# Softmax of a decode attention kernel: per-head exps on ACT replaced by chunked bias adds on DVE, chunked exps on ACT and row sums on PE

## The chip, the cores and the metric

The kernel runs on one core of a Trainium2 chip. The metric is the device time of one execution in microseconds (us). The kernel before takes 427.28 us (median of the 16 runs made beside the changed kernel; 426.35 to 429.26).

Engines: PE is the matmul engine (PEld its weight load), DVE the vector engine, ACT the scalar engine, POOL the general engine, SP the one that issues the DMAs here. "Clock" is the share of full speed that the throttle granted to PE. SBUF is the on-chip memory that the DMA transfers fill; PSUM is the one that PE writes its results to, in pieces called banks. The DMA engines move the data from the main memory (HBM).

## The reference

One token is decoded. It takes attention over a cache of 65,536 positions with 4 key/value heads, each shared by 8 query heads, and adds a small MLP. Keys and values are 2 x 4 x 65536 x 128 bf16, 134 MB of the 170 MB that are read.

```python
q = (x @ wq) ...                                   # 32 query heads of 128
scores = jnp.einsum("bhqd,bhkd->bhqk", q, k) * (Dh ** -0.5)
p = _softmax(scores, axis=-1)
o = jnp.einsum("bhqk,bhkd->bhqd", p, v)
return x + o.reshape(...) @ wo + mlp(...)          # cut
```

## The kernel before

A group is one key/value head with its 8 query heads (`G = 8`). Each group has 16 K chunks and 16 V chunks of 1 MB. A K chunk is transposed on PE in four bank steps; DVE or ACT copies each bank to SBUF; PE multiplies it by q. The scores of a group stay in SBUF as `S_sb[128, 8, 512]`. When all are there, the row max is formed, exp is taken, and the V chunks of the group are multiplied while the K chunks of the next group stream in. The last group has no K chunks to hide behind: at the end of the kernel come four V chunks of group 2 and sixteen of group 3. I call that the tail.

Transfers go through rings of buffers. SP issues them in program order; each waits until PE has used up what its slot held before.

```python
NBK, NBV, NBW = 4, 4, 6            # slots of 1 MB for K, V and weights
...
def dma_chunk(ring, nslots, dst_fn, src, name, allow_sw=False):
    # takes the slot of this ring that has been free for longest
    ...
    o = plan.op("sp", lambda e: e.dma_start(out=dst_fn(slot), in_=src), waits=[prev], ...)
```

A generator issues the softmax of a group between the K steps of the next one. `yield n` lets n steps of other work into the queues first. PE's matmuls start in the order of its queue in these traces, so what stands there behind a wait, waits too (4.0 us in the timeline below).

```python
def stats_chain(g):
    o1 = plan.op("dve", ...tensor_reduce max...)            # row max per partition
    yield 1
    o2 = plan.op("pe", ...transpose of the max...)
    o3, o4 = ...                                            # DVE: max over partitions, diagonal
    yield 1
    o5 = plan.op("pe", ...broadcast of -max to all partitions...)
    o6 = plan.op("dve", ...negb...)
    for h in range(G):                                      # eight exps, one per head
        a.activation(out=P_sb[ss][:, :, h, :], in_=S_sb[ss][:, h, :], func=ACTF.Exp,
                     bias=negb[:, ss, h:h + 1], scale=SCALE, accum_out=lsum[:, ss, h:h + 1])
    yield 3
    o7 = plan.op("pe", ...ones x lsum..., waits=exps + ...) # row sums over partitions
    o8 = plan.op("dve", ...reciprocal...)
...
def v_chunk(g, c, vslot, d_ev):
    waits = [d_ev, need(("exp_done", g))] + ev[("exps", g)]  # all eight exps
    ... # 8 matmuls of 512 columns into O_ps
    release("v", vslot, o)
    if c == NCH - 1: ... # copy O_ps, select (osel), normalise; then the wo matmuls
```

Of the kernel before, what the change touches and what calls it, by code (L numbers as in the profile page):

```python
# [5 lines left out]
ACTF = mybir.ActivationFunctionType  # L6
# [88 lines left out]
def bass_parallel_sum__gqa_block_cached__mixer_s_mlp__decode_kernel(  # L95
# [46 lines left out]
    NDUM0 = 0  # L142
    WCOLS = max(4096, 4 * D, F)
# [5 lines left out]
    with ExitStack() as ctx:  # L149
# [11 lines left out]
        P_sb = [sb(f"p{i}", [128, NT // 16, G, 16], BF16) for i in range(2)]  # L161
        O_sb = sb("o_sb", [128, 512], F32)
        ident_b = sb("ident_b", [128, 128], BF16)
# [4 lines left out]
        band = sb("band", [128, G], F32)  # L168
        valm = sb("valm", [128, 1], mybir.dt.int32)
        m3 = sb("m3", [128, 1], mybir.dt.int32)  # L170
        mb = sb("mb", [128, 4], F32)
        sel = sb("sel", [128, 4, G], F32)
        x8 = sb("x8", [NBD, 128], BF16)
# [18 lines left out]
        lsum = sb("lsum", [128, 2, G], F32)  # L192
# [22 lines left out]
        assert HO + NBF <= 512  # L215
# [59 lines left out]
        def e_consts_pool(p):  # L275
            p.memset(ones_f[:], 1.0)
            p.memset(ones_b[:], 1.0)
            p.memset(shT_b[:], 0.0)
            p.memset(diagP[:], 0.0)
            p.memset(pmaxF[:], 0.0)  # L280
            p.memset(finF[:], 0.0)
            p.memset(dmv[:], 0.0)
            p.memset(qblk[:], 0.0)
            p.memset(selq[:], 1.0)
            return p.memset(band[:], 1.0)
# [8 lines left out]
        def e_ident_f(p):  # L294
# [5 lines left out]
        c_band1 = plan.op("pool", lambda p: p.affine_select(out=band[:], in_=band[:], pattern=[[-16, G]],  # L300
                                                            compare_op=ALU.is_ge, fill=0.0, base=0,
                                                            channel_multiplier=1),
                          waits=[c_pool0], name="band1")
        c_band2 = plan.op("pool", lambda p: p.affine_select(out=band[:], in_=band[:], pattern=[[16, G]],
                                                            compare_op=ALU.is_ge, fill=0.0, base=15,
                                                            channel_multiplier=-1),
                          waits=[c_band1], name="band2")
        c_valm = plan.op("pool", lambda p: p.iota(valm[:], pattern=[[1, 1]], base=0, channel_multiplier=1),
                         name="valm")
        c_selq = None  # L310
        for e in range(2):
# [3 lines left out]
        c_m3 = plan.op("dve", lambda v: v.tensor_single_scalar(out=m3[:], in_=valm[:], scalar=3,  # L315
                                                               op=ALU.bitwise_and),
                       waits=[c_valm], name="m3", cost=0.1)
        c_mb = []
        for b in range(4):
            c_mb.append(plan.op("dve", lambda v, b=b: v.tensor_scalar(out=mb[:, b:b + 1], in0=m3[:], scalar1=float(b),  # L320
                                                                      scalar2=None, op0=ALU.is_equal),
                                waits=[c_m3], name=f"mb{b}", cost=0.1))
        c_sel = None
        for b in range(4):
            c_sel = plan.op("dve", lambda v, b=b: v.tensor_scalar(out=sel[:, b, :], in0=band[:], scalar1=mb[:, b:b + 1],
                                                                  scalar2=None, op0=ALU.mult),
                            waits=[c_band2, c_mb[b]], name=f"sel{b}", cost=0.1)
# [108 lines left out]
        kstate = {"n": 0, "pending_qk": []}  # L436
# [4 lines left out]
        def pe_dummies(n):  # L441
            if n <= 0:
                return

            def e(pe):
                for _ in range(n):
                    last = pe.matmul(O_ps[:], ident_b[:], dmv[:], start=True, stop=True)
                return last
            plan.op("pe", e, waits=[c_ident_b, c_pool0], banks=[BANK_O], name="warm")
# [84 lines left out]
        def stats_chain(g):  # L534
            ss = g % 2
            o1 = plan.op("dve", lambda v: v.tensor_reduce(out=pmaxF[:, 0:G],  # L536
                                                          in_=bms[:, ss, :, :].rearrange("p j h -> p h j"),
                                                          axis=AX.X, op=ALU.max),
                         waits=ev[("bmax", g)] + [c_pool0, ev.get(("pmaxT", g - 1))], name=f"pmax{g}", cost=0.1)
            ev[("pmax_done", g)] = o1  # L540
            yield 1
            o2 = plan.op("pe", lambda pe: pe.transpose(M_ps[:, M_TR:M_TR + 128], pmaxF[:], ident_f[:]),  # L542
                         waits=[o1, c_ident_f], banks=[BANK_M], name=f"pmaxT{g}")
            ev[("pmaxT", g)] = o2
            o3 = plan.op("dve", lambda v: v.tensor_reduce(out=ngm[0:G, :], in_=M_ps[0:G, M_TR:M_TR + 128], axis=AX.X,
                                                          op=ALU.max, negate=True),
                         waits=[o2, ev.get(("diag", g - 1))], banks=[BANK_M], name=f"ngm{g}", cost=0.1)
            o4 = plan.op("dve", lambda v: v.tensor_scalar(out=diagP[0:G, :], in0=ident_f[0:G, 0:G],
                                                          scalar1=ngm[0:G, :], scalar2=SCALE,
                                                          op0=ALU.mult, op1=ALU.mult),  # L550
                         waits=[o3, c_ident_f, c_pool0, ev.get(("negbmm", g - 1))], name=f"diag{g}", cost=0.1)
            ev[("diag", g)] = o4
            yield 1
            o5 = plan.op("pe", lambda pe: pe.matmul(M_ps[:, M_NB:M_NB + G], ones_f[:], diagP[:], start=True,
                                                    stop=True),
                         waits=[o4, c_pool0], banks=[BANK_M], name=f"negbmm{g}")
            ev[("negbmm", g)] = o5
            o6 = plan.op("dve", lambda v: v.tensor_copy(negb[:, ss, :], M_ps[:, M_NB:M_NB + G]),  # L558
                         waits=[o5, ev.get(("exp_done", g - 2))], banks=[BANK_M], name=f"negb{g}", cost=0.1)
            exps = []  # L560
            pw = []
            if g >= 2:
                pw.append(need(("pv_done", g - 2)))
            for h in range(G):
                def e_exp(a, h=h):
                    return a.activation(out=P_sb[ss][:, :, h, :], in_=S_sb[ss][:, h, :], func=ACTF.Exp,  # L566
                                        bias=negb[:, ss, h:h + 1], scale=SCALE, accum_out=lsum[:, ss, h:h + 1])
                exps.append(plan.op("act", e_exp, waits=[o6] + ev[("sevac", g)] + pw + [ev.get(("rl", g - 2))],
                                    name=f"exp{g}_{h}", cost=0.72))
            ev[("exp_done", g)] = exps[-1]  # L570
            ev[("exps", g)] = exps
            yield 3
            o7 = plan.op("pe", lambda pe: pe.matmul(M_ps[:, M_LS:M_LS + G], ones_f[:], lsum[:, ss, :], start=True,  # L573
                                                    stop=True),
                         waits=exps + [c_pool0], banks=[BANK_M], name=f"lsmm{g}")
            o8 = plan.op("dve", lambda v: v.reciprocal(out=rl[:, ss, :], in_=M_ps[:, M_LS:M_LS + G]),
                         waits=[o7, ev.get(("oTn", g - 2))], banks=[BANK_M], name=f"rl{g}", cost=0.1)
            ev[("rl", g)] = o8

        def v_chunk(g, c, vslot, d_ev):  # L580
            ss = g % 2
            waits = [d_ev, need(("exp_done", g))] + ev[("exps", g)]
            ocol = slice(OO + g * G, OO + (g + 1) * G)
            NBLK = NCH - ndirect(g)
            if c >= NBLK:
                def e_pv(pe):
                    for l in range(KL):
                        t = c * KL + l
                        last = pe.matmul(A_ps[:, ocol], Vbuf[vslot][:, l, :], P_sb[ss][:, t // 16, :, t % 16],
# [3 lines left out]
            else:  # L593
                def e_pvb(pe):
                    for q4 in range(KL // 4):
                        t0 = c * KL + 4 * q4
                        w16 = (t0 // 16) * 16
                        last = pe.matmul(O_ps[:], P_sb[ss][:, w16 // 16, :, :].rearrange("p h r -> p (h r)"),  # L598
# [3 lines left out]
                o = plan.op("pe", e_pvb, waits=waits, banks=[BANK_O], name=f"pvb{g}_{c}")  # L602
# [4 lines left out]
            release("v", vslot, o)  # L607
            if c == NCH - 1:
                last_pe = o
# [180 lines left out]
        def v_item(g, c):  # L790
            slot, d_ev = dma_chunk("v", NBV, lambda s: Vbuf[s][:].rearrange("p l d -> p (l d)"), v_view[g, c],
                                   f"dma_v{g}_{c}", allow_sw=True)
            v_chunk(g, c, slot, d_ev)
# [48 lines left out]
        for it in items:  # L842
# [10 lines left out]
            elif it[0] == "flushqk":  # L853
                flush_qk()
        flush_qk()
# [72 lines left out]
```

## Time and profile before

| | kernel before |
|---|---|
| time, median | 427.28 us |
| span of the profiled run | 425.2 us |
| HBM read | 169.87 MB |
| busy: PE, DVE, ACT, POOL | 84%, 30%, 29%, 1% |

The rows below are from the page of the kernel before: the span in 40 slices of 10.6 us each, clock and DMA in tenths of full, and GB/s moved in each slice.

```profile
PEclk9975699667579999999899999888999998899985
DMA  8999999999799999999999999999999999899995
GB/s 328 422 405 403 421 416 417 419 410 405 318 381 425 422 419 418 413 411 420 418 418 423 419 419 414 410 422 422 418 418 423 421 405 392 347 344 427 405 400 202
```

DMA is the limit. It moves about 418 GB/s wherever nothing stops it, and it falls away in four places: at the start, in slices 11 and 12 (the **mid dip**), in slices 34 to 36 (the **tail dip**) and at the end. Windows of 2 us show the two dips closely. The columns after the window are its length, the busy time of PE, PEld, DVE, ACT and POOL (with instruction counts), then clock, DMA share and GB/s.

```profile
112.00:114.00 2.00, 2.00 (x16) 1.94 (x17) 0.66 (x2) 0.00 (x0) 0.00 (x0) 0.50 0.80 336
114.00:116.00 2.00, 2.00 (x30) 1.88 (x29) 1.09 (x3) 0.00 (x0) 0.00 (x0) 0.50 0.31 131
...
360.00:362.00 2.00, 2.00 (x8) 0.80 (x7) 0.00 (x0) 0.39 (x2) 0.00 (x0) 0.77 0.62 258
...
372.00:374.00 2.00, 2.00 (x11) 0.88 (x10) 0.00 (x0) 0.00 (x0) 0.00 (x0) 1.00 0.60 176
```

I measure a dip by its **shortfall**: the sum over the 2 us windows of (418 - GB/s) x 2 / 418, which is the time that DMA would have needed for the bytes that it did not move. From 100 to 130 us it is 3.6 us, from 340 to 400 us it is 4.7 us.

Why the mid dip? This is the timeline at the end of group 0 (start, duration, what; in brackets how long the engine had been idle, and for whom):

```profile
102.89 0.48 PE L542 MATMUL M<-ident_f,pmaxF 128*128 128x128 f32 x1 [2.10 <-DVE pmaxF L536]
...
111.11 0.71 ACT L566 ACTIVATE p<-s,negb 128x512 bf16<-128x512 f32 x1
...
111.97 0.59 PE L573 MATMUL M<-lsum,ones_f 128*128 128x8 f32 x2 [3.97 <-ACT p L566]
```

PE stood for 2.1 us before the row max, and for 4.0 us before the row sums, which need all eight exps. No K slot came free meanwhile, and DMA ran out of slots a little later.

Why the tail dip? This is the timeline around the change from group 2 to group 3 (SPq: SP issues a transfer):

```profile
357.55 7.01 PE L598 MATMUL O<-vbuf,p 128*128 128x512 bf16 x24 [3.15 <-DMA vbuf<-in_A_v_cache_dram]
364.60 0.69 DVE L604 COPY o_sb<-O 128x512 f32<-128x512 f32 x1 [9.99 <-PE O L598]
365.35 1.06 PE L613 MATMUL A<-sel,o_sb 128*128 128x8 f32 x8 [0.79 <-DVE o_sb L604]
366.75 1.78 PE L679 MATMUL A<-oTn_b,wbuf 128*128 128x1 bf16 x64
368.40 7.78 PE L598 MATMUL O<-vbuf,p 128*128 128x512 bf16 x29
...
371.67 0.33 SPq L421 DMA_DIRECT2D vbuf<-in_A_v_cache_dram  x1
```

The last V chunk of group 2 ends at 364.6 us, the first of group 3 starts at 368.4.

The groups of exp instructions (line, operation, shapes, count; busy time and mean ns; idle before):

```profile
L566 ACT ACTIVATE p<-s,negb 128x512 bf16<-128x512 f32 x32 | 22.6, 708 | 7.7 <-DVE negb L558 7.7
L566 ACT ACTIVATION_READ_ACCUMULATOR p<-s,negb 128x1 f32 x32 | 6.0, 186 | 0.0
```

### The profile page before, as it was taken

Reading aid. Unit: us, or ns where it says so; the run is one execution under the profiler, and the core shown is the slowest. Engines: PE = TensorE matmul, PEld = TensorE weight load, DVE = VectorE, ACT = ScalarE, POOL = GpSimd, SP = SyncE. Lnnn points to the kernel's source line nnn. Section 1 sums busy time; section 2 is a strip of 40 time slices with the busy share of each in tenths; the row PEclk is TensorE's granted clock in tenths of the full one; section 3 lists DMA queues with packets and bytes.
Section 4 is the critical chain, followed back from the end, with each engine's and each line's share of the span. In section 5 each row is a group of like instructions: output and inputs, shape, how many; then the busy total and the mean of one; then the engine's idle time right before and its main releaser. Section 6 shows DMA issues by size and latency. Waiting matters only on the chain.

```text
span 425.2 us, 10399 instructions
## 1 busy us (share of the span) xinstructions
PE 358.1 (84%) x4764; PEld 278.4 (65%) x4764; DVE 126.6 (30%) x236; ACT 122.9 (29%) x233; POOL 3.3 (1%) x21
## 2 busy tenths in 40 slices
PE   2767998897699999879999998798999985977484
PEld 2657898887597878656787766577786662532153
DVE  2121444334253333443243333442343341100000
ACT  2222344243532323252233332522233225000000
POOL 3000000000000000000000000000000000000000
PEclk9975699667579999999899999888999998899985
DMA  8999999999799999999999999999999999899995
GB/s 328 422 405 403 421 416 417 419 410 405 318 381 425 422 419 418 413 411 420 418 418 423 419 419 414 410 422 422 418 418 423 421 405 392 347 344 427 405 400 202
DMA packets 30860, 170.55 MB, mean 401 GB/s; under 512 B 2656, under 2 KB 2656, under 8 KB 13408
## 3 DMA queue, kind: packets, MB, share of 16 engines
q1 hardware_dynamic: 30800, 169.88, 98.0%
q8 instruction: 37, 0.61, 0.6%
q14 instruction: 7, 0.06, 0.0%
q10 hardware_dynamic: 16, 0.00, 0.0%
HBM read 169.87 MB, written 0.00 MB: 399 GB/s over the span
## 4 chain that ended last, share of the span: by engine, by line
PE 49%; DMA 44%; ACT 3%; DVE 2%; SPq 1%; issue 1%
DMA kbuf<-in_A_k_cache_dram 28%; PE T L459 22%; PE O L598 16%; DMA vbuf<-in_A_v_cache_dram 11%; PE S L504 7%; ACT p L566 3%; DMA wbuf<-in_A_wq_dram 3%; DMA wbuf<-in_B_w_dram 2%; PE A L679 1%; PE A L613 1%; SPq L421 1%; DVE o_sb L604 0%; PE A L646 0%; PE A L667 0%; PE A L655 0%
## 5 line engine op out<-in xcount | busy, mean ns | idle before, releaser
L459 PE MATMUL T<-ident_f,kbuf 128*128 128x128 f32 x1024 | 180.7, 306 | 12.5 <-DMA kbuf<-in_A_k_cache_dram 12.3
L475 ACT ACTIVATE kt<-T 128x512 f32<-128x512 f32 x151 | 90.2, 597 | 208.3 <-PE T L459 205.1
L459 PEld LDWEIGHTS T<-ident_f,kbuf 128*128 128x128 f32 x1024 | 124.6, 155 | 25.6 <-DMA kbuf<-in_A_k_cache_dram 20.3
L598 PE MATMUL O<-vbuf,p 128*128 128x512 bf16 x504 | 125.7, 397 | 15.5 <-DMA vbuf<-in_A_v_cache_dram 15.5
L471 DVE COPY kt<-T 128x1024 bf16<-128x1024 bf16 x105 | 72.6, 692 | 174.1 <-PE T L459 174.0
L504 PEld LDWEIGHTS S<-qblk,kt 128*128 128x128 bf16 x2048 | 92.5, 100 | 5.9 <-DVE qblk L737 1.0
L598 PEld LDWEIGHTS O<-vbuf,p 128*128 128x128 bf16 x504 | 46.6, 101 | 72.3 <-DMA vbuf<-in_A_v_cache_dram 20.2
L504 PE MATMUL S<-qblk,kt 128*128 128x16 bf16 x2048 | 90.5, 171 | 0.9 <-DVE qblk L737 0.9
L518 DVE COPY s<-S 128x512 f32<-128x512 f32 x32 | 22.0, 686 | 14.6 <-PE S L504 14.6
L566 ACT ACTIVATE p<-s,negb 128x512 bf16<-128x512 f32 x32 | 22.6, 708 | 7.7 <-DVE negb L558 7.7
L524 DVE TENSOR_REDUCE bms<-S 128x8 f32<-128x512 f32 x32 | 21.8, 681 | 0.0
L604 DVE COPY o_sb<-O 128x512 f32<-128x512 f32 x4 | 2.8, 692 | 56.3 <-PE O L598 56.3
L866 ACT ACTIVATE out_b<-M 8x128 bf16<-8x128 f32 x1 | 0.3, 266 | 63.0 <-PE M L864 63.0
L634 PE MATMUL A<-xnT_b,wbuf 128*128 128x1 bf16 x256 | 7.8, 165 | 4.8 <-DMA wbuf<-in_A_wq_dram 3.2
L634 PEld LDWEIGHTS A<-xnT_b,wbuf 128*128 128x128 bf16 x256 | 7.8, 104 | 5.2 <-DMA wbuf<-in_A_wq_dram 3.5
L667 PE MATMUL A<-hT_b,wbuf 128*128 128x1 bf16 x224 | 7.2, 165 | 3.8 <-issue 2.1
L667 PEld LDWEIGHTS A<-hT_b,wbuf 128*128 128x128 bf16 x224 | 6.5, 102 | 4.2 <-issue 2.1
L573 PE MATMUL M<-lsum,ones_f 128*128 128x8 f32 x8 | 1.7, 290 | 7.9 <-ACT p L566 7.9
L542 PE MATMUL M<-ident_f,pmaxF 128*128 128x128 f32 x4 | 1.5, 365 | 8.0 <-DVE pmaxF L536 8.0
L679 PE MATMUL A<-oTn_b,wbuf 128*128 128x1 bf16 x256 | 7.0, 163 | 1.2 <-DVE oTn_b L620 1.0
L679 PEld LDWEIGHTS A<-oTn_b,wbuf 128*128 128x128 bf16 x256 | 6.8, 96 | 1.4 <-issue 1.4
L655 PE MATMUL A<-ln3T_b,wbuf 128*128 128x1 bf16 x224 | 6.8, 164 | 0.0
(84 smaller groups left out, 68.2 us busy)
## 6 DMA issues: line engine op xcount, KB each, us to landing
kbuf<-in_A_k_cache_dram SPq DMA_DIRECT2D x64, 1024.0 KB, 14.9
vbuf<-in_A_v_cache_dram SPq DMA_DIRECT2D x64, 1024.0 KB, 14.8
wbuf<-in_B_w_dram SPq DMA_DIRECT2D x10, 1024.0 KB, 16.7
wbuf<-in_A_wq_dram SPq DMA_DIRECT2D x8, 1024.0 KB, 13.7
wbuf<-in_A_wo_dram SPq DMA_DIRECT2D x8, 1024.0 KB, 19.7
wbuf<-in_B_w_dram SPq DMA_DIRECT2D x8, 896.0 KB, 13.3
wbuf<-in_B_w_dram SPq DMA_DIRECT2D x2, 512.0 KB, 10.7
x<-in_A_x_dram ACTq DMA_DIRECT2D x1, 2.0 KB
```

Source lines behind the costliest of these rows:

```text
L459: last = pe.transpose(T_ps[tb][:, pi * 128:(pi + 1) * 128], Kbuf[kslot][:, l0:l0 + 2, :].rearrange("p t d -> p (t d)").bitcast(F32), ident ...
L471: o_ev = plan.op("dve", lambda v, slot=slot, tb=tb: v.tensor_copy(KT_sb[slot][:], T_ps[tb][:].bitcast(BF16)), waits=waits, banks=[BANK_T[t ...
L475: o_ev = plan.op("act", lambda a, slot=slot, tb=tb: a.activation(out=KT_sb[slot][:].bitcast(F32), in_=T_ps[tb][:], func=ACTF.Copy), waits= ...
L504: last = pe.matmul(o, KT_sb[slot][:, pi * 256 + e:(pi + 1) * 256:2], qblk[:, e, g, :], start=(e == 0), stop=(e == 1))
L518: o1 = plan.op("dve", lambda v: v.tensor_copy(S_sb[ss][:, :, j * SB_T:(j + 1) * SB_T], S_ps[sbank][:].rearrange("p t h -> p h t")), waits= ...
L524: o2 = plan.op("dve", lambda v: v.tensor_reduce(out=bms[:, ss, j, :], in_=S_ps[sbank][:].rearrange("p t h -> p h t"), axis=AX.X, op=ALU.ma ...
L566: return a.activation(out=P_sb[ss][:, :, h, :], in_=S_sb[ss][:, h, :], func=ACTF.Exp, bias=negb[:, ss, h:h + 1], scale=SCALE, accum_out=ls ...
L598: last = pe.matmul(O_ps[:], P_sb[ss][:, w16 // 16, :, :].rearrange("p h r -> p (h r)"), Vbuf[vslot][:, 4 * q4:4 * q4 + 4, :].rearrange("p ...
L634: last = pe.matmul(A_ps[:, QO + hq:QO + hq + 1], W[:, hq * 128:(hq + 1) * 128], xnT_b[:, c:c + 1], start=False, stop=False, skip_group_che ...
L655: last = pe.matmul(A_ps[:, HO + fb:HO + fb + 1], W[:, fb * 128:(fb + 1) * 128], ln3T_b[:, c:c + 1], start=False, stop=False, skip_group_ch ...
L667: last = pe.matmul(A_ps[:, OUTO + nb:OUTO + nb + 1], Wv[:, fi, nb * 128:(nb + 1) * 128], hT_b[:, fb:fb + 1], start=False, stop=False, skip ...
L679: last = pe.matmul(A_ps[:, OUTO + nb:OUTO + nb + 1], Wv[:, hh, nb * 128:(nb + 1) * 128], oTn_b[:, hq:hq + 1], start=False, stop=False, ski ...
```

## The change

The intent is to take exp out of PE's way. The bias is added by DVE for all eight heads at once, in four chunks of 128 score columns; ACT then takes exp of each chunk without bias or accumulator, so V can start after the first chunk. P becomes tile-major, and two matmuls per V chunk give the row sums. The max transposition and the bias broadcast are issued later (3 and 2 steps instead of 1 and 1), so that PE need not stand before them. In the tail, two dummy matmuls per V chunk are to hold the clock up (in the changed kernel it was 0.5 from 365.3 to 372.1 us all the same).

The diff, cut to its core (constants, selection masks and their set-up are left out):

```diff
+    NDUMT = 2
-        P_sb = [sb(f"p{i}", [128, NT // 16, G, 16], BF16) for i in range(2)]
+        PPAD = 12
+        P_sb = [sb(f"p{i}", [128, NT + PPAD, G], BF16) for i in range(2)]
+        St_sb = sb("st", [128, NT, G], F32)
...
+            for i in range(2):
+                p.memset(P_sb[i][:], 0.0)          # POOL, ahead of the constants' signal
...
-            yield 1
+            yield 3
             o2 = ...transpose of the max...
-            yield 1
+            yield 2
             o5 = ...broadcast...
-            for h in range(G):  ...exp per head, accum_out=lsum...
-            yield 3
-            o7 = ...row sums...; o8 = ...reciprocal...
+            for hf in range(NH):                   # NH = 4
+                o_sub = ...v.tensor_tensor(out=St_sb[:, r0:r1, :],
+                                           in0=S_sb[ss][:, :, r0:r1].rearrange("p h t -> p t h"),
+                                           in1=negb[:, ss, :].unsqueeze(1).to_broadcast([128, r1 - r0, G]),
+                                           op=ALU.add)
+                o_exp = ...a.activation(out=P_sb[ss][:, r0:r1, :]..., in_=St_sb[:, r0:r1, :]...,
+                                        func=ACTF.Exp, scale=SCALE)
+                yield 1
...
         def v_chunk(g, c, vslot, d_ev):
-            waits = [d_ev, need(("exp_done", g))] + ev[("exps", g)]
+            waits = [d_ev] + [need(("exp_half", g, hf)) for hf in range(hf_need + 1)]
...
+            o_l16 = ...two matmuls: P windows x ones -> row sums...
             if c == NCH - 1:
+                o_ls = ...DVE lsel...; o7 = ...PE row sums...; o8 = ...DVE reciprocal...
...
         def v_item(g, c):
+            if kstate["done"]:                     # after the last K chunk
+                pe_dummies(NDUMT, tail=True)
```

## The prediction

> **What bounds it now.** DMA. 169.87 MB are read; the page's 40-slice table shows the 16 DMA engines at 0.9 or more nearly everywhere and about 417 GB/s where nothing stops them. In 2 us windows the flow breaks in four places: the start (about 2.3 us lost); 112 to 124 us (131 and 139 GB/s at worst; summing the shortfall against 418 GB/s, 3.6 us lost); 360 to 378 us (176 to 369 GB/s; 4.1 us lost); and from 420.5 us to the end (4.7 us). PE is second: a K chunk plus a V chunk takes PE 4.39 us warm (chain of waits, 131.57 to 135.96) against about 5.0 us of DMA for 2 MB.
>
> **Why the flow breaks.** Buffers are freed by PE. At the end of group 0 (timeline) PE waits 2.1 us for the row max, then 4.0 us (107.9 to 112.0) for all eight exps at the row-sum matmul, at granted clock 0.5; the K buffers run dry behind it. In groups 1 and 2 the same waits (about 2 us for the max; 1.4 us or more for the exps) cause no dip. At the tail the dip comes from cold matmuls at 358 and 368 us (clock 0.5) and the 3.8 us between V of group 2 and V of group 3 (copy, selection, output projection).
>
> **Costs of the change.** Exp now: 8 x 0.72 = 5.76 us of ACT per group. New, per group: four DVE adds of 1024 fp32; [...] an estimate of 1.22 us each, 4.9 us in all; this trace agrees for 512-element work (0.69 us). Four ACT exps, estimate 1.0 to 1.1 us each (now 0.71 us for 512, slope 0.83 ns). [...]
> PE: two row-sum matmuls per V chunk, about 0.1 us (weight-bound ones here pace at 27 to 45 ns), so about 4.5 us per pair, still under DMA. Two 512-column dummies per tail V chunk, about 0.45 us warm: 2.3 us against 2.48 us, little spare.
> POOL: two memsets of 4192 bf16 before the constants' signal, estimate 3.6 us each (512 took 0.53 us): the first projection moves from 9.1 to about 16.4 us. Eight 1 MB loads are already queued to about 22 us, so I expect no lost flow.
>
> **On the critical path.** Group 0: row max and row sums no longer hold PE in order; DVE and ACT are overfull for about four bank steps, so perhaps 2 us of PE stall instead of 6. Gain about 3.3 us of 3.6. Tail: the group-3 max chain is now issued behind V of group 2, so copy, row sum, selection, bias, first add, first exp become serial, estimate 5.4 us instead of 3.8; against that, PE stays warmer and V starts after one of four exps. Gain about 1.5 us of 4.1. Groups 1 and 2, steady state, end: about 0.
>
> Predicted: 423.5 us, 80% range 419.5 to 427.5. Chances: faster by over 2% 0.12, within 2% 0.83, slower 0.05.
>
> **What would show it.** The dip at 112 to 124 us gone; PE no longer waiting for exp at a row-sum matmul; adds near 1.2 us and exps near 1.05 us; tail V period still 2.48 us with clock 1.0; a shortened dip near 360 to 375 us; POOL busy about 10.5 us, DMA not dipping at 20 to 30 us.
>
> **What would make it wrong.** Adds at 2 us or more starving K evacuation (slower); dummies making PE the limit in a cold tail (slower); the late constants opening a head gap; or both dips vanishing entirely (420.5).

## The result

The changed kernel is slower: 429.33 us median (11 runs, 427.91 to 429.98) against 427.28 us. Ratios in this text are the mean time of one kernel's runs over that of the other's runs of the same rounds, so they are not quite the ratios of the medians. Here the ratio is 1.0042 (95% interval 1.0027 to 1.0056). The prediction was 423.5 us, with 427.5 as its upper end.

| | before | after |
|---|---|---|
| time, median | 427.28 | 429.33 |
| span of the profiled run | 425.2 | 425.9 |
| shortfall 100 to 130 us | 3.63 | 0.23 |
| shortfall 340 to 400 us | 4.72 | 8.31 |
| busy: PE, DVE, ACT, POOL | 84%, 30%, 29%, 1% | 86%, 34%, 29%, 2% |

The profiled run of the changed kernel took 427.67 us, less than any of the 11 other runs, so the spans differ by only 0.7 us; I use the profiles for where time goes, and the medians and ratios for how much.

The same rows of the page, after:

```profile
PEclk9995798859589999989699999996999998699985
DMA  8999999999999999999999999999999999699995
GB/s 323 429 400 403 419 419 421 415 412 407 418 411 425 418 419 422 404 417 421 420 403 422 418 420 407 417 421 419 420 422 419 416 407 353 254 341 419 405 403 211
```

Slice 11 is whole now (418 instead of 318), and slice 35 fell from 347 to 254. The windows answer to those above:

```profile
112.00:114.00 2.00, 1.83 (x16) 1.37 (x14) 2.00 (x3) 0.61 (x2) 0.00 (x0) 0.50 1.01 422
114.00:116.00 2.00, 0.47 (x9) 0.47 (x10) 1.09 (x2) 2.00 (x4) 0.00 (x0) 0.50 1.00 414
...
368.00:370.00 2.00, 1.41 (x4) 0.44 (x4) 2.00 (x2) 1.22 (x2) 0.00 (x0) 0.50 0.53 221
370.00:372.00 2.00, 2.00 (x6) 0.76 (x5) 2.00 (x2) 1.23 (x2) 0.00 (x0) 0.50 0.04 16
372.00:374.00 2.00, 2.00 (x13) 0.83 (x11) 1.17 (x1) 1.22 (x2) 0.00 (x0) 0.96 0.36 70
```

The mid dip is gone, as intended. PE's waits in group 0 are shorter than the 2.1 and 4.0 us before:

```profile
103.36 0.33 PE L536 MATMUL M<-ident_f,pmaxF 128*128 128x128 f32 x1 [0.75 <-DVE pmaxF L530]
...
109.35 0.38 PE L498 MATMUL S<-qblk,kt 128*128 128x16 bf16 x8 [1.03 <-ACT kt L469]
...
115.53 0.38 PE L498 MATMUL S<-qblk,kt 128*128 128x16 bf16 x8 [1.70 <-ACT kt L469]
```

From 370 to 372 us DMA moves almost nothing. The new groups:

```profile
L563 DVE TENSOR_TENSOR st<-s,negb 128x1024 f32<-128x1024 f32 x16 | 30.3, 1940 | 0.1
L571 ACT ACTIVATE p<-st 128x1024 bf16<-128x1024 f32 x16 | 16.9, 1057 | 34.8 <-DVE st L563 34.8
L441 PE MATMUL T<-dmv,ident_b 128*128 128x512 bf16 x40 | 12.7, 400 | 0.0
L288 POOL MEMSET p<- 128x4192 bf16 x2 | 7.1, 3594 | 0.0
```

An add takes 1.94 us, not 1.22; an exp takes 1.06 us and waits for its add each time. And the timeline of the change from group 2 to group 3:

```profile
361.13 1.90 PE L604 MATMUL O<-vbuf,p 128*128 128x512 bf16 x8
363.07 0.69 DVE L610 COPY o_sb<-O 128x512 f32<-128x512 f32 x1 [4.21 <-PE A L617]
363.96 0.39 PE L626 MATMUL M<-lsel,ones_f 128*128 128x8 f32 x2 [0.90 <-DVE lsel L622]
365.60 1.84 PE L703 MATMUL A<-oTn_b,wbuf 128*128 128x1 bf16 x64
365.71 7.46 DVE L563 TENSOR_TENSOR st<-s,negb 128x1024 f32<-128x1024 f32 x4
367.70 1.06 ACT L571 ACTIVATE p<-st 128x1024 bf16<-128x1024 f32 x1 [21.77 <-DVE st L563]
368.90 3.48 PE L604 MATMUL O<-vbuf,p 128*128 128x512 bf16 x8 [0.59 <-ACT p L571]
372.41 0.33 SPq L414 DMA_DIRECT2D vbuf<-in_A_v_cache_dram  x1
372.70 1.89 PE L604 MATMUL O<-vbuf,p 128*128 128x512 bf16 x8
```

The last V chunk of group 2 ends at 363.0 us, 1.5 us earlier than before. But the first of group 3 starts at 368.9 us, 0.5 us later than before, runs at half clock for 3.5 us, and its slot is given to the next transfer at 372.41 us instead of 371.67.

To see how far ahead DMA is, I summed the GB/s of the 2 us windows to MB moved since the start:

```
until us     before    changed    b_order   a_mend4     b_late
112           45.40      45.38      45.35     45.36      45.37
130           51.50      52.86      52.91     52.92      52.93
350          143.45     144.62     144.78     144.83     144.84
362          148.08     148.93     148.68     148.71     148.96
372          151.64     151.65     151.70     151.65     151.63
380          154.15     154.13     154.54     154.57     152.95
416          168.95     168.60     169.21     169.15     167.76
```

(The last three columns are experiments, told below; they too have four V slots.) At 130 us the changed kernel is 1.36 MB ahead, which is 3.3 us of DMA: the predicted gain of the mid dip, in full. It keeps most of it until 350 us. By 372 us it has nothing left. All five kernels stand at 151.63 to 151.70 MB there, whatever lead they had. That number can be worked out from the program: after the fourth V chunk of group 3 there follow 12 V chunks, two chunks of wo and 4.19 MB of w4, 18.9 MB in all, and 170.56 - 18.87 = 151.69 MB. DMA has filled all four V slots with group 3 and may not go on before PE has finished the first of them.

### The profile page after: what moved, and what is told of

Read it like the earlier page. It is cut to its first block, busy times and chain, and to the rows that moved or that the text cites. A ratio compares the mean times of both kernels' runs of the same rounds, so it can differ in the third digit from the quotient of the medians.

```text
span 425.9 us, 10698 instructions
## 1 busy us (share of the span) xinstructions
PE 368.1 (86%) x4932; PEld 284.2 (67%) x4932; DVE 144.9 (34%) x232; ACT 125.0 (29%) x201; POOL 10.6 (2%) x23
## 2 busy tenths in 40 slices
DMA packets 30861, 170.56 MB, mean 400 GB/s; under 512 B 2657, under 2 KB 2657, under 8 KB 13409
## 4 chain that ended last, share of the span: by engine, by line
PE 57%; DMA 29%; DVE 7%; POOL 2%; issue 2%; ACT 2%; SPq 1%; POOLq 0%
PE T L453 23%; PE O L604 20%; DMA kbuf<-in_A_k_cache_dram 15%; DMA vbuf<-in_A_v_cache_dram 13%; PE S L498 7%; DVE st L563 4%; POOL p L288 2%; DMA wbuf<-in_B_w_dram 1%; PE A L703 1%; PE A L658 1%; ACT p L571 1%; PE A L637 1%; PE T L441 1%; SPq L414 1%; DVE kt L465 1%
## 5 line engine op out<-in xcount | busy, mean ns | idle before, releaser
L469 ACT ACTIVATE kt<-T 128x512 f32<-128x512 f32 x167 | 99.1, 597 | 189.2 <-PE T L453 186.5
L453 PEld LDWEIGHTS T<-ident_f,kbuf 128*128 128x128 f32 x1024 | 121.1, 154 | 9.0 <-DMA kbuf<-in_A_k_cache_dram 8.6
L465 DVE COPY kt<-T 128x1024 bf16<-128x1024 bf16 x89 | 61.5, 691 | 159.6 <-PE T L453 158.8
L498 PEld LDWEIGHTS S<-qblk,kt 128*128 128x128 bf16 x2048 | 91.4, 100 | 15.9 <-ACT kt L469 8.9
L563 DVE TENSOR_TENSOR st<-s,negb 128x1024 f32<-128x1024 f32 x16 | 30.3, 1940 | 0.1
L571 ACT ACTIVATE p<-st 128x1024 bf16<-128x1024 f32 x16 | 16.9, 1057 | 34.8 <-DVE st L563 34.8
L617 PEld LDWEIGHTS A<-ones_b,p 128*128 128x128 bf16 x128 | 12.8, 100 | 15.9 <-issue 1.9
L441 PE MATMUL T<-dmv,ident_b 128*128 128x512 bf16 x40 | 12.7, 400 | 0.0
L617 PE MATMUL A<-ones_b,p 128*128 128x1 bf16 x128 | 12.3, 166 | 0.0
```

Source lines behind the costliest of these rows:

```text
L441: last = pe.matmul(tgt[:], ident_b[:], dmv[:], start=True, stop=True)
L453: last = pe.transpose(T_ps[tb][:, pi * 128:(pi + 1) * 128], Kbuf[kslot][:, l0:l0 + 2, :].rearrange("p t d -> p (t d)").bitcast(F32), ident ...
L465: o_ev = plan.op("dve", lambda v, slot=slot, tb=tb: v.tensor_copy(KT_sb[slot][:], T_ps[tb][:].bitcast(BF16)), waits=waits, banks=[BANK_T[t ...
L469: o_ev = plan.op("act", lambda a, slot=slot, tb=tb: a.activation(out=KT_sb[slot][:].bitcast(F32), in_=T_ps[tb][:], func=ACTF.Copy), waits= ...
L498: last = pe.matmul(o, KT_sb[slot][:, pi * 256 + e:(pi + 1) * 256:2], qblk[:, e, g, :], start=(e == 0), stop=(e == 1))
L563: return v.tensor_tensor(out=St_sb[:, r0:r1, :], in0=S_sb[ss][:, :, r0:r1].rearrange("p h t -> p t h"), in1=negb[:, ss, :].unsqueeze(1).to ...
```

## The experiments

Theory T: the loss is in the tail. The chain from the last V chunk of group 2 to the first of group 3 got longer, and with four V slots DMA can't run over it. Rival D: the dummy matmuls make PE the limit in the tail. Rival S: the slow adds and the row-sum matmuls cost throughout. Batches of runs share a chip and runs of the kernel before (medians 427.27, 427.58, 427.06 and 427.03 us). Differences between edits of different batches are taken from medians. Every kernel gave a correct result. All were timed in five rounds, with four to six runs of each edit. Where the ratios of two edits are compared below and their intervals overlap, the difference isn't clear of noise. "Shortfall" means mid (100 to 130 us) and tail (340 to 400 us), from the one profiled run of each.

| run | time | ratio to before (95%) | mid | tail |
|---|---|---|---|---|
| changed kernel | 429.33 | 1.0042 (1.0027 to 1.0056) | 0.2 | 8.3 |
| a_early | 427.53 | 1.0009 (0.9988 to 1.0030) | 0.2 | 7.2 |
| a_nodum | 428.59 | 1.0038 (1.0021 to 1.0055) | 0.7 | 8.2 |
| a_tmajor | 428.04 | 1.0023 (1.0006 to 1.0039) | 0.1 | 9.4 |
| a_kslots | 422.09 | 0.9883 (0.9869 to 0.9898) | 0.9 | 0.6 |
| b_kslots | 423.61 | 0.9910 (0.9888 to 0.9931) | 3.4 | 0.5 |
| b_order | 425.36 | 0.9955 (0.9933 to 0.9977) | 0.1 | 7.3 |
| b_rowlate | 425.34 | 0.9955 (0.9929 to 0.9981) | 0.1 | 6.8 |
| a_en | 426.13 | 0.9972 (0.9943 to 1.0002) | 0.2 | 8.1 |
| b_best | 421.85 | 0.9877 (0.9861 to 0.9892) | 0.1 | 0.5 |
| b_best7 | 422.03 | 0.9879 (0.9861 to 0.9896) | 0.1 | 0.5 |
| a_best | 422.03 | 0.9881 (0.9866 to 0.9895) | 0.1 | 1.0 |
| a_pads | 429.06 | 1.0047 (1.0032 to 1.0062) | 0.8 | 8.9 |
| a_mend4 | 426.32 | 0.9990 (0.9971 to 1.0008) | 0.1 | 7.4 |
| b_late | 430.27 | 1.0076 (1.0062 to 1.0090) | 0.1 | 11.0 |

Names that begin with a are edits of the changed kernel, with b of the kernel before.

### a_early: the early chain for the last group

```diff
-            yield 3
+            yield 1 if g == Hkv - 1 else 3
             o2 = ...
-            yield 2
+            yield 1 if g == Hkv - 1 else 2
             o5 = ...
```

> Changed kernel, but for the last group the max transposition and the bias broadcast are issued one step apart as before (1 and 1 instead of 3 and 2), so that they stand ahead of the last V chunks of group 2. Theory T (the loss is the serial chain between V of group 2 and V of group 3): the first add of group 3 starts near 354 us instead of 365.7, no wait for exp at V of group 3, the shortfall of DMA between 340 and 400 us falls from 8.3 us to about 4.5, time about 425.5 us (3.5 to 4 us less than the changed kernel). Rival D (the tail dummies make PE the limit): shortfall stays above 7 us, time within 1 us of 429.3. Rival S (the slow adds and the row-sum matmuls cost throughout): no change, 429.

The first add started at 355.2 us, and PE waited for no exp. The time fell by 1.8 us in the medians (1.4 us by the ratios, whose intervals just overlap), between what T and D had said; the shortfall fell to 7.2 us only, which is what D had said. V of group 3 started at 367.7 us, only 1.2 us earlier than in the changed kernel: copy, row sum, selection and output projection still stood before it, and the dummies. That the order in the last group is a cause is clear of noise only in b_late, below; T had given it too much.

### a_nodum: no dummies

```diff
-    NDUMT = 2
+    NDUMT = 0
```

> Changed kernel without the two dummy matmuls per tail V chunk. Theory T: the chain stays serial, so the gap of about 6 us between the last V chunk of group 2 and the first of group 3 stays; the clock may fall more often; time 428.5 to 431. Rival D: shortfall between 340 and 400 us falls from 8.3 to below 5 us and the time to about 426. Rival S: no change.

The time fell by 0.7 us at most (the intervals overlap), and the tail shortfall stayed at 8.2 us. D is not the cause by itself: without dummies PE simply waited 1.9 us for exp. The dummies did not hold the clock either. With them the first V chunk of group 3 ran at clock 0.5 (3.48 us), without them too (3.19 us for seven of its eight matmuls).

### a_tmajor: scores stored so that the add reads contiguously

```diff
-        S_sb = [sb(f"s{i}", [128, G, NT], F32) for i in range(2)]
+        S_sb = [sb(f"s{i}", [128, NT, G], F32) for i in range(2)]
...
-  v.tensor_copy(S_sb[ss][:, :, j * SB_T:(j + 1) * SB_T], S_ps[sbank][:].rearrange("p t h -> p h t"))
+  v.tensor_copy(S_sb[ss][:, j * SB_T:(j + 1) * SB_T, :], S_ps[sbank][:])
...
-  in0=S_sb[ss][:, :, r0:r1].rearrange("p h t -> p t h")
+  in0=S_sb[ss][:, r0:r1, :]
```

> Changed kernel with the score tile stored tile-major, so that the add reads contiguous floats instead of one float every 2 KB. If the stride is the cause of 1.94 us per add, adds take about 1.22 us [...] and the score copy stays near 0.69 us; if the two fp32 operands or the broadcast are the cause, adds stay near 1.9 us. Theory T: only the first of four adds lies on the tail chain, so it gains about 0.7 us there, perhaps 1 us with what follows: time about 428.3. Rival S (slow adds cost throughout): gains 2 us or more, time 427 or less.

The group of the add in a_tmajor:

```profile
L562 DVE TENSOR_TENSOR st<-s,negb 128x1024 f32<-128x1024 f32 x16 | 18.8, 1219 | 0.1
```

With contiguous reads the same add takes 1.22 us. So the stride, one float every 2 KB, cost 0.72 us per add, 0.70 ns per element. The score copy out of PSUM took 0.68 us (median) both with a step of 32 bytes (before) and contiguous (a_tmajor). The time fell by 1.3 us in the medians (0.8 us by the ratios; the intervals overlap), about what T had said, and S had wanted 2 us or more. (The profiled run was the slowest of its six, 429.38 us, so its shortfall of 9.4 us is no measure of the edit.) So 16 x 0.72 = 11.5 us of DVE time were saved, and little of it was on the critical path.

### a_kslots: eight slots for the tail

By the tail the four K buffers are free. Tail V chunks may use them:

```diff
+            ring, bufs = "v", Vbuf
+            if kstate.get("done") and oldest("k", NBK) < oldest("v", NBV):
+                ring, bufs = "k", Kbuf             # oldest: when the ring's oldest free slot was freed
-            slot, d_ev = dma_chunk("v", NBV, ...Vbuf..., v_view[g, c], ...)
+            slot, d_ev = dma_chunk(ring, len(bufs), ...bufs..., v_view[g, c], ...)
```

> Changed kernel, whose tail V chunks may also use the four K buffers, idle by then: eight slots instead of four. Theory T says that the 6 us stop of PE hurts only because four slots are too few to keep DMA fed over it: with eight, the shortfall between 340 and 400 us falls from 8.3 us to below 2, and the time to about 422.5. Rival D (PE limits by its own work in the tail): the time falls by less than 3 us, since more slots give a slow PE no speed. Rival S: no change.

The time is 422.09 us, 7.2 us less than the changed kernel, and the tail shortfall 0.6 us. PE's stop is still there: its timeline has the last V chunk of group 2 ending at 363.7 us and the first of group 3 starting at 369.6 us, at clock 0.5, with the same chain between them. But DMA runs over it. These are the windows in which the changed kernel had moved 221, 16 and 70 GB/s:

```profile
368.00:370.00 2.00, 1.19 (x8) 0.28 (x7) 2.00 (x2) 1.06 (x1) 0.00 (x0) 0.50 1.04 434
370.00:372.00 2.00, 2.00 (x6) 0.70 (x5) 2.00 (x3) 1.06 (x1) 0.00 (x0) 0.50 0.99 414
372.00:374.00 2.00, 2.00 (x10) 0.89 (x9) 1.84 (x1) 1.18 (x2) 0.00 (x0) 0.74 1.03 430
```

This separates the theories. The dummies, the slow adds and the row sums are all still in this kernel, and it is the fastest of the four. D and S fall as main causes.

After this batch I refined T to T2: each dip is a stop of PE that outlasts the filled slots; the stop in the tail is made of the late chain, the dummies and the row sums, and it costs only because there are four slots.

### b_kslots: the same eight slots in the kernel before

The edit is that of a_kslots.

> Kernel before, with the same eight slots for the tail V chunks and nothing else of the change. Theory T2 (each of the two dips is a PE stop longer than the slots last; they are independent): the mid dip of 3.6 us stays, the tail shortfall falls from 4.7 us to about 0.6, time about 423.3 us. Rival: if eight slots help only because the change made the tail worse, the time stays above 426.

423.61 us, as T2 had said (423.3). The mid dip stays (3.4 us), the tail dip goes (0.5 us). The tail was short of slots before the change as well.

### b_order and b_rowlate: only the issue order of the change

b_rowlate moves the row-sum matmul and the reciprocal behind the last V chunk; b_order also delays the max chain in groups 0 to 2. The eight exps per head stay.

```diff
-            yield 3
-            o7 = ...row sums...; o8 = ...reciprocal...     # in stats_chain
...
             if c == NCH - 1:                               # in v_chunk
+                o7 = ...row sums...; o8 = ...reciprocal...
```
```diff
-            yield 1                                        # b_order only
+            yield 1 if g == Hkv - 1 else 3
...
-            yield 1
+            yield 1 if g == Hkv - 1 else 2
```

> Kernel before with only the issue order of the change: row-sum matmul and reciprocal behind the last V chunk, max transposition and bias broadcast 3 and 2 steps later (1 and 1 in the last group); eight exps per head with accumulated sums on ACT, no add on DVE, no dummies, no row-sum matmuls per chunk. Theory O (what cured the mid dip is the order in PE's queue, not the chunked exp): shortfall between 100 and 130 us falls from 3.6 us to below 0.6, the tail stays at about 4.7, time about 423.8 us. Rival C (the chunked exp is needed, because eight exps in a row hold the copies on ACT): mid shortfall stays above 2 us, time above 425.5.

> Kernel before with only the row-sum matmul and reciprocal moved behind the last V chunk; the max transposition stays one step behind. Theory O: the 4.0 us wait for exp in group 0 goes, the 2.1 us wait for the row max stays; mid shortfall falls from 3.6 us to about 1, time about 424.5 us. If the wait for the max weighs as much, mid shortfall stays above 2 us.

Both cure the mid dip entirely (0.1 us), with the old exps. So what cured it in the changed kernel need not be the chunked exp: it is enough that the row-sum matmul no longer stands in PE's queue in front of the K work. The windows of b_order, to set against those of the kernel before (336 and 131 GB/s):

```profile
112.00:114.00 2.00, 2.00 (x25) 1.88 (x24) 2.00 (x5) 1.09 (x4) 0.00 (x0) 0.58 1.04 434
114.00:116.00 2.00, 2.00 (x38) 1.97 (x37) 1.35 (x3) 0.60 (x1) 0.00 (x0) 1.00 0.99 414
```

The wait for the row max weighs nothing that I could measure: b_rowlate keeps its 8.0 us in all, and is as fast as b_order. C, the rival that the chunked exp is needed, falls.

But both were expected at 423.8 to 424.5 us and took 425.4. Their tail shortfall is 7.3 and 6.8 us, not 4.7. I had not expected that. It is the same thing that the MB table shows: b_order is 1.41 MB ahead at 130 us, and level with the kernel before at 372 us. **A dip that is filled early lets DMA arrive earlier at the next place where slots run out, and wait there longer.** Of the 3.4 us, 2.2 us remain in the medians (1.9 us by the ratio).

### a_en: early chain and no dummies together

Both edits above.

> Changed kernel with both the early chain of the last group and no dummies. Each alone moved the tail little (a_early 8.3 to 7.2 us, a_nodum 8.2): without dummies PE then waited for exp, with the early chain it did the dummies in its backlog. Theory T2: together the tail is like before plus about 1 us for the row sums behind the last V chunk: shortfall 5 to 5.7 us, time about 425.5 us. Rival (something else of the change costs in the tail): shortfall above 7 us, time about 427.5 or more.

426.13 us: 3.2 us less than the changed kernel (3.0 by the ratios). In the medians that is more than a_early (1.8) and a_nodum (0.7) together, but the surplus lies within the noise. The time agrees with T2; the shortfall (8.1 us in the profiled run, which took 427.34 us) agrees with the rival. That run was slower than its median, so its shortfall is the weaker evidence.

### a_pads: only the pads of P set to zero

```diff
-                p.memset(P_sb[i][:], 0.0)
+                p.memset(P_sb[i][:, NT:, :], 0.0)
```

> Changed kernel that sets only the pads of the exp tile to zero (96 elements) instead of all 4192. The first projection moves back from about 16 us to 9 us. If, as predicted, the late constants cost nothing because 8 MB were queued, the time stays within 0.5 us of the changed kernel (429.3); bytes moved by 50 us stay at 19.7 MB. Rival: the head delay is carried to the end, time 2 us or more less.

429.06 us, the same as the changed kernel; the first projection is back at 8.9 us; MB at 50 us 19.71 against 19.69. The 7.1 us of POOL work at the head cost nothing.

### b_best, b_best7, a_best: a version that beats both kernels

b_best is b_order with eight tail slots; b_best7 has seven weight slots too (`NBW = 7`); a_best is the changed kernel with early chain, no dummies, tile-major scores, pads only and eight slots. I also tried the changed kernel with seven weight slots; it did not build (this attempt isn't on record).

> Kernel before with the issue order (row sum late, max chain later except in the last group) and eight tail slots, eight exps per head kept. Theory T2: with eight slots the 1.36 MB (3.3 us) that b_order had gained by 130 us and lost by 372 us is kept to the end, so both gains add: 427.3 - 3.4 - 4.0, time about 420.0 us (419.3 to 421), below a_kslots (422.1), because it has no dummies, no row-sum matmuls and a shorter serial chain. If the chunked exp is worth something by itself once the slots are there, b_best is not faster than a_kslots.

> The same with seven weight slots instead of six. In a_kslots the last weight chunk was issued at 410.9 us only when the output projection freed a slot, and DMA idled from 410 to 416 us. If that issue is on the last chain, seven slots give 1 to 2 us: about 418.8 us. If the end is PE's own chain after the last V chunk, the time is within 0.5 us of b_best.

> Changed kernel with every mend: early chain of the last group, no dummies, tile-major scores, only the pads of the exp tile set to zero, eight tail slots. Theory T2: all PE stops in the tail are covered by the slots, so the mends beyond the slots bring at most 1 to 2 us over a_kslots: about 420.5 us, equal to b_best within 0.7 us. If the added work (row-sum matmuls, adds) costs throughout, it stays above b_best by over 1 us.

All three take 421.9 to 422.0 us, as a_kslots does (422.1). With the slots there and the mid dip cured, nothing else of the change matters: chunked exp or eight exps, dummies or none, fast adds or slow. b_best missed its 420.0 us by 1.9 us, b_best7 its 418.8 by 3.2 and a_best its 420.5 by 1.5; a_best does equal b_best, as expected. Something common seems to limit the end. In b_best the DMA flow thins out after 408 us:

```profile
410.00:412.00 2.00, 1.85 (x70) 1.77 (x68) 0.00 (x0) 0.00 (x0) 0.00 (x0) 0.50 0.72 230
412.00:414.00 2.00, 0.69 (x26) 0.63 (x24) 0.00 (x0) 0.00 (x0) 0.00 (x0) 0.50 0.81 299
414.00:416.00 2.00, 1.01 (x38) 1.01 (x38) 0.00 (x0) 0.00 (x0) 0.00 (x0) 0.50 0.34 130
```

Seven weight slots did not change that, so it is not the weight ring: in b_best7 the last transfer is issued at 405.99 us instead of 409.93, and lands no earlier (417.1 us against 416.9; b_best7's profiled run, 423.0 us, was slower than its median). What it is, I leave open.

### a_mend4 and b_late: what is left over

a_mend4 is a_best without the eight slots. b_late is b_order with 3 and 2 steps in the last group too.

> Changed kernel with the early chain of the last group, no dummies, tile-major scores and only the pads set to zero, but still four tail slots. If the named terms are all of it, it equals b_order: 425.4 us within 0.7. If the chunked exp and the row-sum matmuls cost something that no mend removes, it stays at 426.3 or more (a_en was 426.1 with the slow adds).

> b_order, but with the order of the change in the last group too: max transposition 3 and bias broadcast 2 steps later there as well. Then all eight exps of group 3 (5.8 us) stand between the last V chunk of group 2 and the first of group 3: the gap on PE grows from 4.3 us to about 8 us, and the time from 425.4 to about 429. The chunked exp was then made for this gap: it lets V start after one of four. If the time stays at 425.4, the order in the last group does not matter, and a_early's gain came from elsewhere.

b_late took 430.27 us, 4.9 us more than b_order, as the theory says. Its timeline shows all eight exps between the last V chunk of group 2, which ends at 362.9 us, and the first of group 3:

```profile
365.24 0.72 ACT L566 ACTIVATE p<-s,negb 128x512 bf16<-128x512 f32 x1 [18.73 <-DVE negb L558]
...
370.19 0.70 ACT L566 ACTIVATE p<-s,negb 128x512 bf16<-128x512 f32 x1
371.13 8.79 PE L591 MATMUL O<-vbuf,p 128*128 128x512 bf16 x32 [4.26 <-ACT p L566]
```

So the chunked exp does earn something: with the same late order it is about 1 us faster (429.33 against 430.27, in different batches; 1.4 us by the ratios, whose intervals do not overlap), because V waits for one exp of four. The two kernels differ in the dummies, the adds and the row sums as well, so the size is not that of the chunked exp alone. But the late order in the last group made that wait, and issuing the chain early there avoids it with the old exps as well.

a_mend4 took 426.32 us, 1.0 us more than b_order, which is the second of the two outcomes expected (426.3 or more); the intervals of the ratios overlap. Something small of the chunked form may remain; what, I can't say.

### One number that orders the four-slot kernels

The first V slot that group 3 frees is where DMA starts again. Its issue is one line in each trace:

| kernel | issued at | span | span - issue |
|---|---|---|---|
| b_rowlate | 370.48 | 425.2 | 54.7 |
| a_early | 370.60 | 424.9 | 54.3 |
| b_order | 370.75 | 424.6 | 53.9 |
| a_mend4 | 371.12 | 425.2 | 54.1 |
| before | 371.67 | 425.2 | 53.5 |
| a_en | 371.89 | 425.6 | 53.7 |
| changed | 372.41 | 425.9 | 53.5 |
| a_tmajor | 372.95 | 427.6 | 54.7 |
| a_nodum | 372.98 | 426.2 | 53.2 |
| a_pads | 373.28 | 427.0 | 53.7 |
| b_late | 374.73 | 428.5 | 53.8 |

The last column stays within 53.2 to 54.7 us over eleven kernels, while the mid shortfall ranges from 0.1 to 3.6 us. To 1.5 us, the span of a four-slot kernel is when PE finishes the first V chunk of group 3, plus 54 us. Each row is one profiled run. That of the changed kernel was a lucky one; a_pads, whose tail is the same program and whose profiled run (428.75 us) is near the median, shows V of group 3 starting at 370.0 us and the issue at 373.28.

## Why the prediction was wrong

1. **Bound by DMA, with PE freeing the slots: right.** The shortfalls and the slot experiments rest on it.
2. **"Gain about 3.3 us of 3.6" at the mid dip: right where it arises, wrong as a gain.** The shortfall fell by 3.4 us and DMA was 1.36 MB (3.3 us) ahead at 130 us. By 372 us the lead was gone. The wrong step is that I added the two dips as if each were worth its own shortfall (4.8 us in all, of which the forecast took 3.8). They lie in series, and the second stops DMA at a fixed byte (151.7 MB) until PE has finished a certain chunk. b_order, which has the cure alone, gained 2.2 us.
3. **"Tail: ... Gain about 1.5 us of 4.1": wrong in sign; this is the step that failed.** The shortfall from 340 to 400 us rose from 4.7 to 8.3 us. Most of that rise is the lead being waited out (step 2): b_order, with the mid cure and the old order in the last group, has 7.3 us. What the tail adds is read from the times: the changed kernel is 4.0 us slower than b_order (3.7 by the ratios), and b_late shows that the late order alone costs 4.9 with the old exps. The terms:
   - The serial chain, estimated at 5.4 us, took 5.9 us (363.0 to 368.9). The order was read correctly; the add in it was 1.94 us, not 1.22. I had named adds of 2 us or more as a risk and not used it.
   - "PE stays warmer": no. The clock was 0.5 from 365.3 to 372.1 us in spite of the dummies (before, from 367.8 to 371.2), and the first V chunk of group 3 took 3.48 us; in the kernel before it took 3.08, and a chunk at full clock takes 1.90. Which chunks met the half clock differs from kernel to kernel, so part of this may be luck.
   - "V starts after one of four exps": right, and worth about 1 us (b_late against the changed kernel), but against a wait that the new order itself made. Before the change the exps of group 3 ended at 360.3 us, ahead of need.
   - I compared 5.4 us with 3.8 us and still wrote a gain. I never asked how long four slots last. They ran dry at about 369 us, before the first was freed.
4. **"2.3 us against 2.48 us, little spare" for the dummies: the size was right.** V chunks that were not waiting for DMA came 2.20 us apart, and 2.48 us apart once PE had caught up. But 2.20 us is also how fast a backlog can be worked off; in b_order the chunks came 1.73 us apart. That may be where the dummies cost: a_en, without them, is 1.4 us faster than a_early in the medians, but the intervals overlap, so this isn't shown.
5. **POOL and the head: right.** Each memset took 3.59 us (estimate 3.6), the first projection started at 15.7 us (estimate 16.4), and a_pads shows that it cost nothing.
6. **The engines in group 0: right in kind, the stall mis-sized.** Exps took 1.06 us. PE's waits for ACT's bank copies are new, 1.0 and 1.7 us in group 0; with the 0.75 us that is left for the row max that is 3.5 us, where I had said perhaps 2. DMA did not notice them.

Of the four things that the prediction named as able to make it wrong, none is what happened: the adds came near 2 us but K was not starved (418 GB/s in slice 11), a_nodum and a_pads speak against the dummies and the head, and the dips did not both vanish. The order of issue in the last group was in the sum and not on that list.

Two estimates of the prediction can be set beside the traces. A straight line through two groups of DVE copies in the kernel before (0.167 us for 8 fp32 elements per partition, 0.686 us for 512) gives an estimate of 1.21 us for 1024, near the 1.22 of the prediction; a_tmajor measured 1.219 us. With the strided reads of the changed kernel it did not hold (1.94 us). A line through two groups of ACT in the kernel before (0.177 us for 8 elements, 0.597 us for 512) gives an estimate of 1.02 us for an exp of 1024; measured 1.06 us.

The clock did not follow the length of the last PE gap. In the changed kernel a gap of 2.26 us before the V chunk at 351 us was followed by clock 0.5, and so was one of 2.73 us in b_late at the same place; in the changed kernel the clock fell again at 365.3 us with no gap above 0.90 us in the 9 us before it. In the kernel before, gaps of 2.51 us before 188.0 us and of 3.30 us before 400.3 us left it at 1.0, and so did one of 2.19 us before 351 us in a_tmajor. The length of one gap doesn't decide it in these traces.

What stays open: the thin flow after 408 us in the eight-slot kernels, and whether it is what holds a_kslots and the three best ones at 422 us; and the 1.0 us of a_mend4 over b_order, if it is real.

## What to carry to other kernels

In this kernel, which DMA bounds, a stop of PE cost only what outlasted the filled slots, so count the slots at each stop before shortening the stop: giving idle buffers to the ring was worth 7.2 us here (6.8 by the ratios), and four other mends together 3.0 us (2.2 by the ratios). Gains in series did not add here: ask what the transfer engine will do with a lead when it reaches the next place where slots run out. And look at the order of issue separately in the last stage, where there is no other work to stand between a producer and its user.
